# Output of the MLP by seven quarter products in two more batches, with the operand combinations of w2 kept in DRAM

## Chip, core, metric

One core of one Trainium2 chip (trn2), all data fp32. The metric is device time in microseconds (us) of one execution. The kernel before took 1165.28 us (median of three runs, 1165.25 to 1166.52). "Faster" or "slower" means a difference of over 2%.

The engines: TensorE (PE in the profile, with its weight loads as PEld), VectorE (DVE), ScalarE (ACT), GpSimd (POOL), and SyncE (SP), which here only issues DMA transfers.

## The reference, cut to what matters

```python
# attention of 4 batches x 8 heads, 768 tokens of 64, masked by equal hash buckets -> x (4, 768, 512)
X = np.fft.fft(np.fft.fft(x, axis=1), axis=2)
u = x + np.real(X)
un = (u - mean(u)) / sqrt(var(u) + 1e-6)
return u + np.maximum(un @ w_ch1, 0.0) @ w_ch2      # w1: 512 x 2048, w2: 2048 x 512
```

The kernel works batch by batch (0 to 3) and weaves the attention of the next batch between the mix and MLP of the current one. Most of the MLP is two matrix products: h = relu(w1 x) and o = h w2. The change concerns the second, o.

## The kernel before: the parts concerned

A product of two matrices that are cut 2 x 2 takes eight products of quarters, or seven if combinations of the quarters are formed by additions first. Seven cost TensorE an eighth less and give VectorE additions to do. Each product is summed up in a bank of PSUM; copying or adding it out of the bank, so that the next product can have it, is called evacuation here. The kernel before already computes h by seven quarter products in batches 1 to 3, and o in batch 3 only. Batches 1 and 2 compute o directly; one token tile T of 128 tokens is one accumulation over 8 blocks for each of two halves of the hidden units:

```python
def outer(b, T, u, rs, rows, tag, whole=True):
    ...
        ps = pt([P, w], ...)                       # one PSUM bank of 128 x 512
        for i, (hr, fc) in enumerate(rows):
            nc.tensor.matmul(ps, hr, w2[:, fc, cols], start=(i == 0), stop=(i == len(rows) - 1))
            if i % 4 == 3:
                yield                              # here the attention of the next batch steps in
        nc.vector.scalar_tensor_tensor(            # u += rs * ps: the only work of DVE per tile
            u[:, cols], ps, rs, u[:, cols], op0=ALU.mult, op1=ALU.add)
        if whole:
            store(b, T, u, cols)                   # GpSimd issues the DMA to the output
```

Batch 3 uses `outer7`, for a pair of token tiles (j, j+3) at a time. Its shape, with the seven products named by their operands:

```python
s1 = a21 + a22;  s3 = a11 - a21                # operand sums on DVE, 128 x 512 each
p1 = product(a11, B11)                         # 4 matmuls 128 x 256 into a PSUM bank
qq = copy(p1)                                  # ACT
a11 = s1 - a11                                 # DVE
p4 = product(a22, T4);   v_low  += rv * p4     # evacuation by DVE
p1 = product(a12, B21, p1)                     # accumulates into the bank of the first
u_low += ru * p1                               # DVE
a12 = a12 - a11                                # DVE
pa = product(s1, T1);    p5 = copy(pa)         # ACT
pb = product(s3, T3);    p7 = copy(pb)         # ACT
pb = product(a11, T2)
qq += pb; u_high += ru*qq; qq += p7; v_low += rv*qq; qq += p5; v_high += rv*qq    # DVE
pa = product(a12, B22, pa); u_high += ru * pa  # DVE
```

T1 to T4 are the combinations of w2's quarters. `combine()` formed them in SBUF when batch 3 began (16 additions of 128 x 512). w1's combinations were already handled otherwise: formed once in batch 0 (`quarters`), written to DRAM (`ad`), and fetched block by block into a ring of NR = 12 buffers.

Of the kernel before, what the change touches and what calls it, by code (L numbers as in the profile page):

```python
# [11 lines left out]
F32 = mybir.dt.float32  # L12
# [5 lines left out]
ALU = mybir.AluOpType  # L18
AX = mybir.AxisListType

P = 128
B, H, S, D = 4, 8, 768, 64
# [457 lines left out]
def _main(  # L480
# [27 lines left out]
    def wt(shape, dtype, tag, name, bufs=2):  # L508
        return work.tile(shape, dtype, tag=tag, name=name, bufs=bufs)
# [599 lines left out]
    NR = 12  # L1109
# [12 lines left out]
    side = [w1f[:, at + i * HALF : at + (i + 1) * HALF] for i in range(2)]  # L1122

# [23 lines left out]
    HD = DM // 2  # L1147
    t7 = {}

    def combine():  # L1150
        parts = []
        for tl in (*pks, *(wt([P, 2, S], F32, "t6", f"t7_{i}", 2) for i in range(2))):
            dims = "p a b c -> p (a b c)" if len(tl.shape) == 4 else "p a b -> p (a b)"
            flat = tl.rearrange(dims)
            parts += [
                flat[:, i * 2 * HD : (i + 1) * 2 * HD].rearrange("p (k n) -> p k n", k=2)
                for i in range(3)
            ]
        for half in range(2):
            sums = [[parts.pop() for _ in range(3)] for k in range(2)]  # L1160
            for k in range(2):
                r = half * HF // 2 + 2 * k
                (b11, b12), (b21, b22) = (
                    [w2[:, i : i + 2, n : n + HD] for n in (0, HD)] for i in (r, r + HF)
                )
                t1, t2, t4 = sums[k]
                nc.vector.tensor_tensor(t1, b12, b11, op=ALU.subtract)
                nc.vector.tensor_tensor(t2, b22, t1, op=ALU.subtract)
                nc.vector.tensor_tensor(t4, b21, t2, op=ALU.subtract)
                nc.vector.tensor_tensor(b12, b22, b12, op=ALU.subtract)  # L1170
                for kk in range(2):
                    t7[half, 2 * k + kk] = (
                        b11[:, kk], b21[:, kk], b22[:, kk], t4[:, kk],
                        t1[:, kk], t2[:, kk], b12[:, kk],
                    )

    def outer7(b, half, hall, ut, rs):
        def tile_sums(j):
            if half == 0:
                for T in (j, j + GT):  # L1180
                    rs[T] = spread(b, T, ut[T])
            a11, a12, a21, a22 = (
                hall[:, i, :, (j + g * GT) * P : (j + g * GT + 1) * P]
                for g in range(2) for i in range(2)
            )
            s1 = wt([P, HF // 2, P], F32, "qt", f"s1_{half}_{j}", 2)
            nc.vector.tensor_tensor(s1, a21, a22, op=ALU.add)
            nc.vector.tensor_tensor(a21, a11, a21, op=ALU.subtract)
            return a11, a12, a21, a22, s1

        nxt = tile_sums(0)
        for j in range(GT):
# [4 lines left out]
            def product(a, i, ps=None):  # L1197
                start = ps is None
                if start:
                    ps = pt([P, HD], f"o{b}_{half}_{j}_{i}")  # L1200
                for r in range(HF // 2):
                    nc.tensor.matmul(  # L1202
                        ps, a[:, r], t7[half, r][i], start=start and r == 0,
                        stop=r == HF // 2 - 1, skip_group_check=not start,
                    )
                return ps

            low, high = slice(0, HD), slice(HD, DM)
            tmp = wt([P, 3, HD], F32, "kt", f"tmp{half}_{j}", 2)

            def add(t, r, cols, src):
                nc.vector.scalar_tensor_tensor(
                    t[:, cols], src, r, t[:, cols], op0=ALU.mult, op1=ALU.add
                )


            p1 = product(a11, 0)
# [3 lines left out]
            p4 = product(a22, 3)  # L1221
            add(v, rv, low, p4)
            yield
            p1 = product(a12, 1, p1)
# [4 lines left out]
            pa = product(s1, 4)  # L1229
            nc.scalar.copy(p5, pa)  # L1230
            yield
            pb = product(s3, 6)
# [3 lines left out]
            pb = product(a11, 5)  # L1236
# [11 lines left out]
            pa = product(a12, 2, pa)  # L1248
            add(u, ru, high, pa)
            if half:  # L1250
                store(b, j, u, high)
            yield

    def mlp7(b):
# [4 lines left out]
        if b == B - 1:  # L1259
            combine()  # L1260
# [36 lines left out]
        for half in range(2):  # L1297
# [46 lines left out]
            if b == B - 1:  # L1344
                yield from outer7(b, half, hall, ut, rs)
                continue
            for T in range(NT):
                if half == 0:
                    rs[T] = spread(b, T, ut[T])
                rows = [  # L1350
                    (hall[:, i, r, T * P : (T + 1) * P], i * HF + half * HF // 2 + r)
                    for r in range(HF // 2) for i in range(2)
                ]
                yield from outer(b, T, ut[T], rs[T], rows, f"{half}_", half == 1)
# [3 lines left out]
    MIX += [2 + NT + NDC + 2 * (7 * HF // 4 + NT * HF // 4)] * (B - 1)  # L1358
    LEFT = 8

    def after(n, one, two):

        for i, _ in enumerate(one):
            if i >= n and (i - n) % 5 < 4:
                next(two, None)
            yield

# [25 lines left out]
    for b in range(B):  # L1393
# [41 lines left out]
        if b == 0:  # L1435
            other = after(2 + NT, other, chain(weights(w2, moe_w_ch2), quarters()))
# [47 lines left out]
```

## Time and profile before

| | before |
|---|---|
| time, median of 3 | 1165.28 us |
| profiled execution | 1170.13 us, mean granted clock 0.992 |
| o of batches 1 and 2, TensorE | 192 matmuls 128x512 |
| o of batch 3, TensorE | 168 matmuls 128x256 (seven quarter products) |
| GpSimd-issued transfers | 65 (25 weight reads, 40 output stores) |

The page gives busy time per engine, then the same in 40 slices, then groups of like instructions; its lines for PE, DVE and DMA are in the prediction below. Each fp32 matmul of the source leaves two records in the trace, so 192 matmuls are 384 records.

### The profile page before, as it was taken

Reading aid. Unit: us, or ns where it says so; the run is one execution under the profiler, and the core shown is the slowest. Engines: PE = TensorE matmul, PEld = TensorE weight load, DVE = VectorE, ACT = ScalarE, POOL = GpSimd, SP = SyncE. Lnnn points to the kernel's source line nnn. Section 1 sums busy time; section 2 is a strip of 40 time slices with the busy share of each in tenths; the row PEclk is TensorE's granted clock in tenths of the full one; section 3 lists DMA queues with packets and bytes.
Section 4 is the critical chain, followed back from the end, with each engine's and each line's share of the span. In section 5 each row is a group of like instructions: output and inputs, shape, how many; then the busy total and the mean of one; then the engine's idle time right before and its main releaser. Section 6 shows DMA issues by size and latency. Waiting matters only on the chain. (4 is left out here: it accounts for less than half of the span.)

```text
span 1168.2 us, 12778 instructions
## 1 busy us (share of the span) xinstructions
PE 1120.9 (96%) x4633; PEld 589.3 (50%) x4633; DVE 720.8 (62%) x1225; ACT 438.6 (38%) x822; POOL 63.2 (5%) x133
## 2 busy tenths in 40 slices
PE   7999889999999999999999999999999999999996
PEld 4444355454445445644444444554444444868675
DVE  4889949838447365883457753885634857645353
ACT  6777348623223113344224511345313420251330
POOL 1000001101100010020000000002000001010002
PEclk9999989999999999999999999999999999999999
DMA  9524124404112011022102311013101211130201
GB/s 270 158 68 127 36 71 164 150 4 151 52 41 55 9 32 36 19 70 80 27 19 68 91 36 50 15 46 94 41 1 41 63 32 36 37 96 4 72 19 39
DMA packets 117958, 73.67 MB, mean 63 GB/s; under 512 B 80128, under 2 KB 112000, under 8 KB 117888
## 3 DMA queue, kind: packets, MB, share of 16 engines
q1 hardware_dynamic: 110544, 52.98, 16.8%
q0 software_dynamic: 5776, 19.40, 5.0%
q8 instruction: 39, 0.64, 0.2%
q10 hardware_dynamic: 1568, 0.39, 0.2%
q14 instruction: 31, 0.25, 0.1%
HBM read 59.12 MB, written 13.63 MB: 62 GB/s over the span
## 5 line engine op out<-in xcount | busy, mean ns | idle before, releaser
L1065 PE MATMUL o<-w,h 128*128 128x512 f32 x576 | 254.9, 596 | 0.6 <-DVE rt L859 0.6
L819 ACT ACTIVATE pk<-sc 128x768 f32<-128x768 f32 x192 | 147.8, 808 | 152.0 <-PE sc L815 107.1
L1065 PEld LDWEIGHTS o<-w,h 128*128 128x128 f32 x576 | 106.7, 190 | 132.1 <-issue 125.3
L825 DVE SCALAR_TENSOR_TENSOR pk<-qb,kb,pk 128x768 f32<-128x768 bf16 x132 | 129.4, 1013 | 66.3 <-ACT pk L819 66.3
L815 PE MATMUL sc<-qt,kt 64*128 64x384 f32 x768 | 153.5, 503 | 0.9 <-ACT pk L819 0.9
L836 PE MATMUL oo<-pk,vn 128*64 128x385 f32 (+1 forms) x768 | 150.4, 502 | 1.9 <-DVE pk L825 1.8
L1290 PE MATMUL h_p<-x,w 128*128 128x384 f32 x384 | 140.2, 494 | 2.1 <-ACT qt L531 0.6
L898 DVE TENSOR_TENSOR acc<-acc,pk 128x1536 f32<-128x1536 f32 (+1 forms) x80 | 113.3, 1433 | 9.9 <-ACT pk L819 9.2
L1290 PE MATMUL h_p<-w 128*128 128x384 f32 x288 | 106.3, 492 | 2.9 <-ACT qt L531 1.7
L1290 PEld LDWEIGHTS h_p<-x,w 128*128 128x128 f32 x384 | 69.7, 190 | 56.5 <-ACT h L1322 3.4
L836 PEld LDWEIGHTS oo<-pk,vn 128*64 128x64 f32 x768 | 48.1, 137 | 92.3 <-issue 75.6
L815 PEld LDWEIGHTS sc<-qt,kt 64*128 64x128 f32 x768 | 67.1, 187 | 49.7 <-issue 25.4
L1083 PE MATMUL h<-x,w 128*128 128x384 f32 x256 | 88.6, 499 | 1.0 <-ACT kt L531 0.6
L1290 PEld LDWEIGHTS h_p<-w 128*128 128x128 f32 x288 | 53.1, 190 | 43.4 <-ACT qt L531 2.4
L1083 PEld LDWEIGHTS h<-x,w 128*128 128x128 f32 x256 | 48.1, 193 | 37.4 <-issue 5.0
L1070 DVE SCALAR_TENSOR_TENSOR u<-o,rs,u 128x512 f32<-128x512 f32 x14 | 10.5, 751 | 67.3 <-PE o L1065 61.6
L995 ACT COPY F<-cs 128x257 f32<-128x257 f32 (+1 forms) x32 | 10.9, 377 | 91.4 <-PE cs L988 91.4
L1202 PE MATMUL o<-w,h 128*128 128x256 f32 x192 | 44.7, 379 | 0.0
L1202 PEld LDWEIGHTS o<-w,h 128*128 128x128 f32 x192 | 36.5, 190 | 5.4
L531 ACT COPY qt<-trq 128x192 f32<-128x192 f32 x40 | 14.8, 427 | 61.7 <-DVE qt L529 61.7
L988 PE MATMUL cs<-ch,z 128*128 128x128 f32 (+3 forms) x192 | 32.7, 322 | 4.7 <-ACT kt L531 2.6
L926 POOL DMA_DIRECT2D out_dram<-w x20 | 11.1, 557 | 476.9 <-DVE w L1070 346.3
(169 smaller groups left out, 1261.7 us busy)
## 6 DMA issues: line engine op xcount, KB each, us to landing
w<-ad SPq DMA_DIRECT2D x168, 128.0 KB, 2.0
zraw<-in_moe_w_ch_dram POOLq DMA_DIRECT2D x21, 512.0 KB, 4.2
vn<-in_v_dram SPq DMA_DIRECT2D x32, 192.0 KB, 3.3
qn<-in_q_dram SPq DMA_DIRECT2D x31, 192.0 KB, 3.3
kn<-in_k_dram SPq DMA_DIRECT2D x31, 192.0 KB, 3.4
ad<-st SPq DMA_DIRECT2D x8, 512.0 KB, 3.7
ad<-w SPq DMA_DIRECT2D x24, 128.0 KB, 2.2
fraw<-in_moe_w_ch_dram SPq DMA_DIRECT2D x4, 512.0 KB, 9.2
```

Of the source, the lines that this page charges most:

```text
L531: nc.scalar.copy(dst, src)
L815: last[0] = nc.tensor.matmul(ps[:, h, 0:HALF], kt[rows, ks], qt[rows, qs], start=kb is not None, stop=True,)
L819: nc.scalar.activation(pk[:, g, :, 0:HALF], ps[:, :, 0:HALF], AF.Exp, scale=SCALE)
L825: nc.vector.scalar_tensor_tensor(w, qb[:, h].rearrange("p (g s) -> p g s", g=2), kb[:, h, c : c + 1], w, op0=ALU.is_equal, op1=ALU.mult,)
L836: nc.tensor.matmul(oos[g][h * D : (h + 1) * D, 0:w], nat["v", n][:, c, h, :], pk[:, g, h, 0:w], start=(c == 0), stop=(c == NT - 1),)
L898: nc.vector.tensor_tensor(acc[:, g], (first if c == 1 else acc)[:, g], new[:, g, :, 0:HALF], op=ALU.add,)
L926: nc.gpsimd.dma_start(out[b, s0 : s0 + 2 * w - 1 : 2, cols], src[at : at + w, cols])
L988: nc.tensor.matmul(ps[:, pc + 2 * lo : pc + 2 * hi - 1 : 2], z[:, cp, pc, par, t * P : (t + 1) * P], ch[:, cp, pc, lo:hi], start=(cp == 0) ...
L1065: nc.tensor.matmul(ps, hr, w2[:, fc, cols], start=(i == 0), stop=(i == len(rows) - 1))
L1083: nc.tensor.matmul(ps, w1[:, c, fc * P : (fc + 1) * P], x[:, c, g * HALF : (g + 1) * HALF], start=(c == 0), stop=(c == NDC - 1),)
L1202: nc.tensor.matmul(ps, a[:, r], t7[half, r][i], start=start and r == 0, stop=r == HF // 2 - 1, skip_group_check=not start,)
L1290: nc.tensor.matmul(ps, ring[n % NR][:, k], right[i][:, k], start=start and k == 0, stop=k == 1, skip_group_check=not start,)
```

## The change

The intent: o by seven quarter products in batches 1 and 2 as well. There all seven right operands have to be available three times, and w2 itself and its four combinations don't fit beside each other. So all seven blocks of each half (B11, B21, B22, T1 to T4, 512 KB each) are written to DRAM once, in batch 0 (`quarters2`), and fetched into w2's place for every half pass; the fetch for the next half pass is issued right after a block's last use. The diff, cut to its core:

```diff
-    NR = 12
+    NR = 9
@@ combine() goes, quarters2() comes
+    bd = tc.dram_tile([2, 7, P, HF // 2, HD], F32, name="bd")
+    right7 = [w2f[:, i * QB : (i + 1) * QB]... for i in range(7)]      # seven places in w2
+    def quarters2():
+        st = wt([P, 3, 4, HD], F32, "z", "st2", 1)
+        for half in range(2):
+            for i, rows, n in ((B11, lo, 0), (B21, hi, 0), (B22, hi, HD)):
+                nc.sync.dma_start(bd[half, i], w2[:, rows, n : n + HD])      # the plain copies
+            for r in range(HF // 2):
+                ...                                                        # t1 .. t4 on DVE, 128 x 256
+                nc.sync.dma_start(bd[half, T4:, :, r]..., st[:, r % 3])
+                yield
@@ outer7
+                if j == GT - 1 and (b < B - 1 or half == 0):
+                    nc.sync.dma_start(right7[i], bd[1 - half, i])
             if j < GT - 1:
                 nxt = tile_sums(j + 1)
-            pb = product(a11, 5)
+            def third():
+                add(u, ru, high, product(a12, B22, pa))
+            if b < B - 1:          # in batches 1 and 2 this product comes before a11 * T2
+                third()
+                yield
+            pb = product(a11, T2)
@@ mlp7
-            if b == B - 1:
-                yield from outer7(b, half, hall, ut, rs)
-                continue
-            for T in range(NT): ... yield from outer(...)
+            yield from outer7(b, half, hall, ut, rs)
@@ batch 0
-            other = after(2 + NT, other, chain(weights(w2, moe_w_ch2), quarters()))
+            other = after(2 + NT, other, chain(weights(w2, moe_w_ch2), quarters(), quarters2()))
```

More of the change, by code (lines that the diff above doesn't have):

```diff
@@ L1122, in _main @@
     side = [w1f[:, at + i * HALF : at + (i + 1) * HALF] for i in range(2)]
+    HD = DM // 2
+    temps = [
+        w1f[:, at + i * S : at + (i + 1) * S].rearrange("p (i n) -> p i n", n=HD)
+        for i in range(2)
+    ]
     def quarters():
@@ L1142, in quarters @@
             yield
-    HD = DM // 2
-    t7 = {}
-    def combine():
-        parts = []
-        for tl in (*pks, *(wt([P, 2, S], F32, "t6", f"t7_{i}", 2) for i in range(2))):
-            dims = "p a b c -> p (a b c)" if len(tl.shape) == 4 else "p a b -> p (a b)"
-            flat = tl.rearrange(dims)
-            parts += [
-                flat[:, i * 2 * HD : (i + 1) * 2 * HD].rearrange("p (k n) -> p k n", k=2)
-                for i in range(3)
-            ]
+    B11, B21, B22, T4, T1, T2, T3 = range(7)
+    bd = tc.dram_tile([2, 7, P, HF // 2, HD], F32, name="bd")
+    w2f = w2.rearrange("p c f -> p (c f)")
+    QB = HF // 2 * HD
+    right7 = [
+        w2f[:, i * QB : (i + 1) * QB].rearrange("p (r n) -> p r n", n=HD) for i in range(7)
+    ]
+    s1s = [
+        w2f[:, 7 * QB + i * HD * 2 : 7 * QB + (i + 1) * HD * 2].rearrange(
+            "p (r n) -> p r n", n=P
+        )
+        for i in range(2)
+    ]
+    def quarters2():
+        st = wt([P, 3, 4, HD], F32, "z", "st2", 1)
         for half in range(2):
-            sums = [[parts.pop() for _ in range(3)] for k in range(2)]
-            for k in range(2):
-                r = half * HF // 2 + 2 * k
+            lo, hi = (slice(i + half * HF // 2, i + (half + 1) * HF // 2) for i in (0, HF))
+            for i, rows, n in ((B11, lo, 0), (B21, hi, 0), (B22, hi, HD)):
+                nc.sync.dma_start(bd[half, i], w2[:, rows, n : n + HD])
+            for r in range(HF // 2):
                 (b11, b12), (b21, b22) = (
-                    [w2[:, i : i + 2, n : n + HD] for n in (0, HD)] for i in (r, r + HF)
+                    [w2[:, i + half * HF // 2 + r, n : n + HD] for n in (0, HD)]
+                    for i in (0, HF)
                 )
-                t1, t2, t4 = sums[k]
+                t4, t1, t2, t3 = (st[:, r % 3, i] for i in range(4))
                 nc.vector.tensor_tensor(t1, b12, b11, op=ALU.subtract)
@@ L1169, in combine @@
                 nc.vector.tensor_tensor(t4, b21, t2, op=ALU.subtract)
-                nc.vector.tensor_tensor(b12, b22, b12, op=ALU.subtract)
-                for kk in range(2):
-                    t7[half, 2 * k + kk] = (
-                        b11[:, kk], b21[:, kk], b22[:, kk], t4[:, kk],
-                        t1[:, kk], t2[:, kk], b12[:, kk],
-                    )
+                nc.vector.tensor_tensor(t3, b22, b12, op=ALU.subtract)
+                nc.sync.dma_start(
+                    bd[half, T4:, :, r].rearrange("i p n -> p i n"), st[:, r % 3]
+                )
+                yield
     def outer7(b, half, hall, ut, rs):
@@ L1185, in tile_sums @@
             )
-            s1 = wt([P, HF // 2, P], F32, "qt", f"s1_{half}_{j}", 2)
+            s1 = s1s[j % 2]
             nc.vector.tensor_tensor(s1, a21, a22, op=ALU.add)
@@ L1202, in product @@
                     nc.tensor.matmul(
-                        ps, a[:, r], t7[half, r][i], start=start and r == 0,
+                        ps, a[:, r], right7[i][:, r], start=start and r == 0,
                         stop=r == HF // 2 - 1, skip_group_check=not start,
                     )
+                if j == GT - 1 and (b < B - 1 or half == 0):
+                    nc.sync.dma_start(right7[i], bd[1 - half, i])
                 return ps
             low, high = slice(0, HD), slice(HD, DM)
-            tmp = wt([P, 3, HD], F32, "kt", f"tmp{half}_{j}", 2)
+            tmp = temps[j % 2]
             def add(t, r, cols, src):
@@ L1214, in add @@
                 )
-            p1 = product(a11, 0)
+            p1 = product(a11, B11)
             qq, p5, p7 = (tmp[:, i] for i in range(3))
@@ L1220, in outer7 @@
             nc.vector.tensor_tensor(a11, s1, a11, op=ALU.subtract)
-            p4 = product(a22, 3)
+            p4 = product(a22, T4)
             add(v, rv, low, p4)
             yield
-            p1 = product(a12, 1, p1)
+            p1 = product(a12, B21, p1)
             add(u, ru, low, p1)
@@ L1228, in outer7 @@
             nc.vector.tensor_tensor(a12, a12, a11, op=ALU.subtract)
-            pa = product(s1, 4)
+            pa = product(s1, T1)
             nc.scalar.copy(p5, pa)
             yield
-            pb = product(s3, 6)
+            pb = product(s3, T3)
             nc.scalar.copy(p7, pb)
@@ L1247, in outer7 @@
             yield
-            pa = product(a12, 2, pa)
-            add(u, ru, high, pa)
+            if b == B - 1:
+                third()
+                yield
             if half:
                 store(b, j, u, high)
-            yield
     def mlp7(b):
@@ L1258, in mlp7 @@
         )
-        if b == B - 1:
-            combine()
+        if b == 1:
+            for i in range(7):
+                nc.sync.dma_start(right7[i], bd[0, i])
         t1, t2, t4 = bs
@@ L1343, in mlp7 @@
                     yield
-            if b == B - 1:
-                yield from outer7(b, half, hall, ut, rs)
-                continue
-            for T in range(NT):
-                if half == 0:
-                    rs[T] = spread(b, T, ut[T])
-                rows = [
-                    (hall[:, i, r, T * P : (T + 1) * P], i * HF + half * HF // 2 + r)
-                    for r in range(HF // 2) for i in range(2)
-                ]
-                yield from outer(b, T, ut[T], rs[T], rows, f"{half}_", half == 1)
+            yield from outer7(b, half, hall, ut, rs)
     MIX = [2 + NT + NDC + 2 * (NFC + GT * NFC // 4)]
-    MIX += [2 + NT + NDC + 2 * (7 * HF // 4 + NT * HF // 4)] * (B - 1)
+    MIX += [2 + NT + NDC + 2 * (7 * HF // 4 + GT * 4)] * (B - 1)
     LEFT = 8
@@ L1366, in after @@
             yield
+        for _ in two:
+            pass
     other = weights(w1, moe_w_ch1)
```

## The prediction

> **What bounds the kernel now.** I read the page's busy shares and slices first, then the chain of waits, then stretches of the time by engine, then the timeline inside the stage that changes. The chain that ended last is of no use here: it holds only the last output transfer. Busy shares and slices:
>
> ```profile
> PE 1120.9 (96%) x4633; PEld 589.3 (50%) x4633; DVE 720.8 (62%) x1225; ACT 438.6 (38%) x822; POOL 63.2 (5%) x133
> ...
> PE   7999889999999999999999999999999999999996
> PEld 4444355454445445644444444554444444868675
> DVE  4889949838447365883457753885634857645353
> ...
> DMA  9524124404112011022102311013101211130201
> ```
>
> PE (TensorE) is at nine tenths or more in nearly every slice, DVE (VectorE) nowhere near that for long, DMA idle after the start. So the sum of TensorE's work sets the time, and what is not TensorE work counts only where it makes TensorE wait. The stretch of batches 1 and 2, with the tail (columns: stretch, us, then busy us of each engine):
>
> ```profile
> 491.90:766.00 274.10, 267.69 (x1064) 130.24 (x1063) 166.26 (x263) 96.97 (x180) 10.54 (x21) 1.00 0.19 50
> 766.00:1000.00 234.00, 230.71 (x847) 110.02 (x846) 142.56 (x235) 75.88 (x143) 10.54 (x21) 1.00 0.15 44
> ...
> 548.00:610.00 62.00, 61.91 (x215) 26.08 (x212) 28.91 (x39) 13.50 (x22) 0.00 (x0) 1.00 0.09 20
> 671.00:735.00 64.00, 63.49 (x230) 29.27 (x226) 32.08 (x55) 13.48 (x24) 4.56 (x9) 1.00 0.14 39
> ```
>
> The last two rows are the two halves of batch 1's output product o (before: full 128x512 matmuls) with the attention of batch 2 woven in. TensorE idles 0.6 us of 126 there, and DVE is busy 61 of 126: there is little waiting to win, only work, and DVE has about half its time free. What one matmul really costs is the distance between starts, not the mean of the group list, since they overlap:
>
> ```profile
> 692.83 27.73 PE L1065 MATMUL o<-w,h 128*128 128x512 f32 x64
> ...
> 720.40 1.05 PE L988 MATMUL cs<-ch,z 128*128 128x129 f32 x8
> ```
> ```profile
> 1055.21 1.89 PE L1202 MATMUL o<-t,s 128*128 128x256 f32 x8
> ...
> 1056.94 1.89 PE L1202 MATMUL o<-w,h 128*128 128x256 f32 x8
> ```
>
> From the first pair (720.40 - 692.83) / 64 = 0.431 us for one 512-wide record; from the second, in batch 3 which already uses seven products, (1056.94 - 1055.21) / 8 = 0.216 us for a 256-wide one. Each matmul of the source leaves two such records (batch 3: 2 halves x 3 tile pairs x 7 products x 4 = 168 matmuls; its groups count 192 + 48 + 48 + 24 + 24 = 336).
>
> **What the Trainium skill says.** "TensorE: Matmul & The Clock Gate", section Back-to-back issue gap, gives 518 cycles for 512 columns and 262 for 256: two halves cost only 1% more than one whole. The trace agrees (2 x 0.216 = 0.432 against 0.431), at twice the time per record because the data are fp32. "Perfetto Trace Analysis", section Identifying the Most-Contended Engine, says that matmul busy time is a poor measure of the distance to the limit; hence the starts above. Its section Matmuls wants independent groups to rotate through PSUM banks so that the evacuation of one overlaps the next: this is the point on which my prediction turns, because in batches 1 and 2 only two banks serve these products (batch 3 has six). "VectorE: DVE Perf Modes", section The TRN2 errata, gives (N+151)/0.96 ns for an fp32 add; 691 ns for 512 and 424 ns for 256. The trace has 690 ns and 416 to 425 ns.
>
> **The change part by part.**
> TensorE, batches 1 and 2. Removed per batch: 2 halves x 6 tiles x 8 = 96 matmuls, 192 records x 0.429 (0.431 with one attention switch or two) = 82.4 us. Added: 168 matmuls, 336 records x 0.216 = 72.6 us. Gain 9.8 us a batch, 19.6 us in both: 1.7% of 1165.3. That is all the arithmetic can give, and it is entirely on the bounding engine.
>
> DVE, batches 1 and 2. Per pair of tiles and half the old form has two 128x512 updates of 0.75 us. The new one has four 128x512 adds (0.69), six 128x256 scaled updates (0.483) and three 128x256 adds (0.42): 2.76 + 2.90 + 1.27 = 6.92 us against 1.50, so +5.4 us; six of them a batch: +32.5 us, +65 us in both. ACT gets three copies of 0.37 each: +13 us in both. Beside TensorE this fits: the stretch 548 to 610 becomes about 57 us long with 28.9 + 16.3 = 45.2 us of DVE (79%); 671 to 735 about 59 us with 48.4 (82%). So DVE doesn't become the bound on average, but its queue gets full.
>
> Forming the combinations. The sixteen-fold 128x512 work of `combine` (16 x 0.69 = 11 us of DVE, around 967 to 985) goes. In its place 32 adds of 128x256 (32 x 0.42 = 13.4 us of DVE) come in batch 0's mix, after the like combinations of w1 at about 293 us, where DVE is busy 9.2 and 6.1 of 20 us: hidden. Both were off the bounding engine, so about 0.
>
> Transfers. Written once: 14 blocks of 512 KB, 7.3 MB. Fetched: 7 blocks for each of six half passes, 42 x 512 KB = 22 MB. 512 KB lands in 3.7 to 4.4 us here; seven in a row are at most some 31 us. The block of the next half is asked for as soon as its last use in this half is over, and the h products in between last 61 us (610 to 671) in batches 1 and 2 and 37 us in batch 3; for batch 1 the place in w2 is free from 446 us and needed at 548. So hidden. The ring of w1 blocks falls from 12 to 9 places of 128 KB: at 4 records x 0.323 = 1.3 us a product that is still 11 us ahead of a landing of 2.0 us. Cost 0 to 2 us where a 512 KB block is queued in front.
>
> PSUM banks. This is the term that I have to estimate. The old outer product holds a bank for 16 records (6.9 us), and its evacuation may come up to 6.9 us late without harm. A quarter product is 8 records, 1.73 us; with two banks the evacuation of one must be done when the next ends. Four of the five evacuations per tile pair are DVE's, and DVE is in order behind the attention's work. One attention step in this stage, from the same trace:
>
> ```profile
> 580.99 1.56 PE L815 MATMUL sc<-qt,kt 64*128 64x384 f32 x8
> ...
> 583.55 1.95 DVE L825 SCALAR_TENSOR_TENSOR pk<-qb,kb,pk 128x768 f32<-128x768 bf16 x2 [5.14 <-ACT pk L819]
> ...
> 585.89 1.75 DVE L898 TENSOR_TENSOR acc<-acc,pk 128x1536 f32<-128x1536 f32 x1
> ```
>
> DVE is taken until 587.64, 6.65 us after the step began; TensorE is through with the step's own matmuls after 2.9 us. Two quarter products bring it to 6.4 us, then the third wants the first one's bank, which DVE frees at about 6.65 + 0.48 + 0.2 = 7.3. Depending on which of the four steps of a tile pair follows, I get 0, about 0.7, 0.3 to 1.9, and 0.6 us of waiting: some 0.5 us a step. An output stage is 24 of some 56 steps that are spread over 24 attention steps, so 10 attention steps a batch, less those left for the end: 18 in both batches, 18 x 0.5 = 9 us. I add 1 us for the transfers.
>
> Sum: -19.6 + 9 + 1 = about -10 us, 1155 us.
>
> **The rivals.** (a) Nothing waits: the scheduled order puts the evacuations ahead of the attention's adds, and the whole 19.6 us come out: 1146. For it: the h products live on the same two banks with 1.3 us of slack and the long stretch 491.9 to 766 shows TensorE idle only 6.4 us. Against it: those banks are emptied by ACT, whose queue is short there. (b) Evacuation on a full DVE takes the place of the work removed: 1 us or more per attention step and several at the normalising of a head pair (690.8 to 696.3, DVE without a break), 20 us or more: 1165 or slower. For it: DVE at 80% with pieces of up to 1.75 us against a slack of 1.73. Against it: the attention's own matmuls, 2.9 us, often stand between two quarter products and give DVE time. (c) The fetches come late: 512 KB blocks in front of the ring or of q, k and v: a wait of several us at six half passes, 1160 to 1175. Against it: DMA is at 0.09 to 0.19 of its capacity here. (d) More than the arithmetic: only if the shorter DVE-heavy stretch before batch 3 also gains; I see no more than 1 to 2 us.
>
> **Range and chances.** The floor is 1144 to 1146, no waits; I put the low end at 1146. The upper end is waits of 18 us, 1164. Faster by over 2% means below 1142, more than all the removed work: 2%. Slower by over 2% means above 1188.6, 42 us of waits: 3%. Within 2%: 95%.
>
> **What would show it.** Right: no 128x512 output records after batch 0, 1008 quarter records at 0.216 us apart; TensorE's busy time down by less than 20 us; DVE up by some 65 us; short TensorE gaps of 0.3 to 2 us inside the output stages of batches 1 and 2, released by DVE's scaled updates, none in batch 3; time in the h stages unchanged. Wrong: gaps before the quarter products that end with a transfer (rival c); no gaps at all (a); gaps that add up to over 18 us (b); a longer batch 0, which would mean that forming the combinations isn't hidden.

## The result, and the profile after

| | before | after |
|---|---|---|
| median of the runs taken together | 1165.9 us (1165.25 to 1170.73, 4 runs) | 1154.97 us (1154.21 to 1155.47, 4 runs) |
| ratio of the fast runs | | 0.9897, 95% interval 0.9869 to 0.9924: within 2% |
| output correct | yes | yes |

A ratio is the mean time of one kernel's fast runs over that of the other's of the same rounds, so it isn't quite the ratio of the medians quoted beside it.

The page after, with the lines that answer to those of before:

```profile
PE 1100.6 (96%) x4921; PEld 641.9 (56%) x4921; DVE 779.9 (68%) x1373; ACT 451.8 (39%) x858; POOL 74.5 (6%) x149
...
DVE  4889959837938455883857877785775877644352
...
DMA  9534135514611014113042315013104204131401
...
L1214 PE MATMUL o<-w,h 128*128 128x256 f32 x864 | 194.0, 381 | 0.0
...
w<-bd SPq DMA_DIRECT2D x42, 512.0 KB, 4.4
```

TensorE is busy 20 us less and DVE 59 us more than on the page before. (Against the second trace of before, introduced below, in which TensorE was busy 1115.8 us, it is 15 us less; busy time is not the work, as the prediction says.) The added DVE work shows in the slices of batches 1 and 2 (20th to 34th). The 42 fetches of `bd` land in 4.4 us (median). All of that is near what was predicted (for DVE, some 65 us). What the page doesn't tell is whether the total of about -10 us came about in the predicted way, as -19.6 + 9 + 1. For that I compared traces.

First, a caution about which traces. The first trace of before is of a long execution (1170.13 us). I took a second one of the same kernel later (run `d0_before_trace`, 1165.16 us). Two stretches of both, in batch 0; columns are the stretch, its length, busy us of PE, PEld, DVE, ACT, POOL with instruction counts, then PEclk, the share of full TensorE clock that was granted:

```profile
150.00:162.00 12.00, 9.32 (x43) 4.87 (x43) 4.96 (x5) 4.83 (x10) 0.00 (x0) 0.72 0.37 87
224.00:242.00 18.00, 15.98 (x53) 8.66 (x53) 11.74 (x20) 9.38 (x20) 1.05 (x2) 0.91 0.34 114
```
```profile
150.00:162.00 12.00, 9.39 (x61) 5.73 (x60) 5.78 (x7) 5.71 (x12) 0.00 (x0) 1.00 0.28 67
224.00:242.00 18.00, 17.34 (x66) 9.24 (x67) 9.33 (x18) 6.84 (x13) 1.05 (x2) 1.00 0.27 81
```

The first fence is the long execution, the second the short one. PEclk (the third number from the end) is below 1 in the long one alone. The records there show the clock at one half for 3.4 us, or twice that: 6.8 us at half clock in 12 us gives 0.72, 3.4 us in 18 gives 0.91. A further 3.4 us at half clock, at 128 us, are in both executions. The Trainium skill, "TensorE: Matmul & The Clock Gate", section What's actually happening, says that TensorE's clock is halved after an idle window of about 3.4 us and that this window runs freely, without being reset when a kernel starts. The traces agree on the length and on the free running: in the first one the halved stretches begin at 129.02, 152.91 and 228.01 us, 7 and 22 times 3.41 us apart, and the same kernel meets them in other places from run to run. They don't agree that the window is idle: in the 3.4 us before these three beginnings TensorE's records cover 34%, 46% and 41% of the time. Of the 35 runs of the kernel before whose clock is on record, the 13 with mean clock 0.998 took 1164.5 to 1165.5 us and the 8 with 0.992 took 1169.5 to 1170.7. The two traces account for it: 13.6 us at half clock are 6.8 us of lost clock, 3.4 us are 1.7, and the two executions are 5.0 us apart. (The mean clock also counts time at half clock after the last matmul, 4.6 us of it in `d0_before_trace`, which costs nothing.) So I compare traces that have these stretches in the same places, or name the difference.

The cleanest pair is `d0_before_trace` against the second trace of after (`c0_after_again`, 1155.26 us): both have one half-clock stretch, at 128 us, before the difference begins. The attention's score matmuls are the same 768 records in both kernels, so the start of the n-th one is a clock for comparing them:

| start of score record n | before, us | after, us | difference | where this is |
|---|---|---|---|---|
| 256 | 188.2 | 188.5 | +0.3 | batch 0, ahead of its MLP |
| 288 | 258.3 | 263.4 | +5.1 | batch 0, in its MLP |
| 480 | 550.5 | 556.0 | +5.5 | batch 1, o begins |
| 512 | 600.9 | 602.4 | +1.5 | half of o of batch 1 |
| 640 | 761.8 | 759.3 | -2.5 | between the o stages |
| 736 | 908.0 | 901.3 | -6.7 | batch 2, ahead of the second half of o |
| last matmul | 1153.5 | 1142.3 | -11.2 | end of batch 3 |
| end of span | 1163.2 | 1153.4 | -9.8 | |

Each of the four half stages of o gives 4.0 to 4.5 us. But 5 us are lost in batch 0, where nothing was predicted, and 1.4 us after the last matmul. The sum comes out right because its errors cancel. The rest of the work was to find out what each of the three pieces is.

**The o stages.** I added up, in the traces, the distance from each output record of batches 1 and 2 to the next TensorE record. Before: 384 records, 167.9 us, of which 384 x 0.429 = 164.8 are the floor and 3.1 are extra. After: 672 records, 151.6 us, of which 672 x 0.216 = 145.2 are the floor and 6.5 extra. So the work fell by 19.6 us, the prediction's number, but the extra grew by only 3.4 us where it had 9 us of waits. Not all of the 3.4 is waiting: 2.6 us, in seven places of both batches, end with one of DVE's scaled updates; the rest is more of the 0.1 us steps that stand in both kernels at changes to or from the attention's matmuls. The load of DVE in the first half stage of batch 1, `d0_before_trace` and then after, and under it the last half stage of batch 2 in after:

```profile
543.40:600.80 57.40, 57.30 (x190) 24.30 (x188) 26.58 (x36) 10.96 (x18) 0.00 (x0) 1.00 0.09 21
```
```profile
547.60:601.40 53.80, 53.45 (x262) 37.77 (x260) 38.05 (x62) 13.79 (x27) 0.00 (x0) 1.00 0.24 72
...
932.70:975.90 43.20, 43.03 (x205) 34.18 (x204) 33.18 (x70) 6.18 (x14) 7.03 (x13) 1.00 0.25 83
```

DVE is busy 38.05 of 53.80 us, 71%; the prediction had 79% for this stage. But the waits don't simply follow this load: the four half stages have loads of 71, 75, 71 and 77% and extras of 1.9, 1.9, 1.8 and 0.9 us, so the fullest one has the least. What TensorE's output products waited for in the whole kernel after (columns: who ended the idle time, us, times):

```profile
L1214 PE MATMUL o<-w,h x864: 379/379/483, 547.7 to 1141.3; 128*128 128x256 f32 x173
...
its engine sat idle before it (us, times) until:
  issue: 4.6, 8
  DVE u L1226: 2.3, 2
...
  DVE w L1226: 1.6, 4
```

At most six waits of these products end with one of DVE's scaled updates (L1226). The list counts weight loads and matmuls separately, so one wait can be in it twice. The largest one lies behind the normalising of a head pair, where the prediction had seen DVE without a break:

```profile
691.28 0.55 DVE L869 TENSOR_TENSOR x<-x,rb 128x384 f32<-128x384 f32 x1
691.75 1.01 DVE L825 SCALAR_TENSOR_TENSOR pk<-qb,kb,pk 128x768 f32<-128x768 bf16 x1
692.68 0.48 DVE L1226 SCALAR_TENSOR_TENSOR u<-o,rs,u 128x256 f32<-128x256 f32 x1
...
693.21 1.99 PE L1214 MATMUL o<-w 128*128 128x256 f32 x8 [0.93 <-DVE u L1226]
```

DVE runs the attention's instructions one after the other (each starts before the one ahead of it has ended: 691.75 + 1.01 is later than 692.68), and only then the update that frees the bank. In an ordinary attention step it is the other way round:

```profile
577.14 1.95 DVE L825 SCALAR_TENSOR_TENSOR pk<-qb,kb,pk 128x768 f32<-128x768 bf16 x2 [1.50 <-ACT pk L819]
...
577.50 1.99 PE L1214 MATMUL o<-w 128*128 128x256 f32 x8
...
579.12 1.76 DVE L898 TENSOR_TENSOR acc<-acc,pk 128x1536 f32<-128x1536 f32 x1
...
579.33 3.62 PE L1214 MATMUL o<-w,h 128*128 128x256 f32 x16
...
579.55 0.36 ACT L1244 COPY w<-o 128x256 f32<-128x256 f32 x1
581.26 0.37 ACT L1247 COPY w<-o 128x256 f32<-128x256 f32 x1 [1.35 <-PE o L1214]
...
582.99 0.48 DVE L1226 SCALAR_TENSOR_TENSOR w<-o,rs,w 128x256 f32<-128x256 f32 x1 [2.11 <-PE o L1214]
```

This is the step for which the prediction assumed some 0.5 us of waiting. Three quarter products (8 + 16 records) run on without a gap while DVE masks and adds for 3.7 us; the first two are emptied by ACT. Then DVE itself stands idle for 2.11 us until TensorE is done.

**Batch 0.** In the trace of after, between 226 and 237 us, DVE, then TensorE:

```profile
228.18 0.69 DVE L607 SCALAR_TENSOR_TENSOR w<-zraw,w 128x512 int32<-128x512 int32 x1
230.93 0.43 DVE L603 TENSOR_SCALAR w<-zraw 128x512 int32<-128x512 int32 x1 [2.06 <-DMA zraw<-in_moe_w_ch_dram]
...
234.01 0.43 DVE L603 TENSOR_SCALAR w<-zraw 128x512 int32<-128x512 int32 x1 [1.45 <-DMA zraw<-in_moe_w_ch_dram]
...
235.56 0.55 DVE L1089 TENSOR_SCALAR h<-h 128x384 f32<-128x384 f32 x1
```
```profile
236.16 6.15 PE L1083 MATMUL h<-x,w 128*128 128x384 f32 x13 [3.13 <-DVE h L1089]
```

DVE waits twice for a transfer that brings weights (zraw). Behind that in its queue is the relu of h (L1089), and TensorE waits 3.13 us for it. In before (`d0_before_trace`) the same wait was 0.66 us:

```profile
233.36 5.43 PE L1083 MATMUL h<-x,w 128*128 128x384 f32 x16 [0.66 <-DVE h L1089]
```

What stands in those transfers' way is on SP's queue, again in after:

```profile
225.20 1.24 SPq L1173 DMA_DIRECT2D bd<-w  x2
...
274.41 1.25 SPq L1173 DMA_DIRECT2D bd<-w  x2
```

These are four of the six plain copies of w2's quarters to DRAM (L1173); the first two are issued at 188.7 and 208.8 us. In the program they come after `quarters()`, but they need nothing but w2, so they were scheduled as soon as the rows they read were there, between the last reads of weights. GpSimd issues the last two weight reads at 224.78 and 226.32 us; two copies of 512 KB each are issued from 225.20 us on. From issue to landing, these two reads take 6.1 and 7.7 us; in `d0_before_trace` they take 5.1 and 4.9, and in d2 below, where the copies come later, 4.6 each. And the wait has a second price. The stretches around it, for after:

```profile
224.00:232.00 8.00, 7.78 (x24) 4.48 (x24) 4.94 (x11) 4.14 (x9) 1.06 (x2) 1.00 0.81 234
232.00:236.20 4.20, 1.07 (x10) 0.20 (x9) 2.75 (x6) 1.56 (x4) 0.00 (x0) 1.00 0.39 148
236.20:242.00 5.80, 5.80 (x13) 3.36 (x14) 0.38 (x1) 0.49 (x1) 0.00 (x0) 0.71 0.00 0
```

The DMA share (the number after PEclk) is 0.81 where it is 0.60 in `d0_before_trace`; then TensorE is idle for 3.1 of 4.2 us; then its clock is halved for 3.4 us, which makes 0.71 over 5.8 us and costs another 1.7 us. A wait of 3.1 us became a loss of about 5.

**The end.** After the last matmul nothing differs but the end of GpSimd's program: a drain instruction of its sequencer, visible in the trace though not in the views, takes 5381 ns before and 6765 ns after. GpSimd issued 65 transfers before and 81 after. The group of output stores in the page after:

```profile
L926 POOL DMA_DIRECT2D out_dram<-w x30 | 16.5, 552 | 468.7 <-issue 426.6
```

with 26 more that store from u. 56 stores and 25 weight reads are 81. Before there were 40 stores, because a tile was stored as one piece of 512 columns; seven quarter products finish the two column halves apart, and the change stores them apart.

### The profile page after: what moved, and what is told of

The parts are those of the page before. It is cut to its first block, busy times and chain, and to the rows that moved or that the text cites. A ratio compares the mean times of both kernels' runs of the same rounds, so it can differ in the third digit from the quotient of the medians.

```text
span 1152.4 us, 13749 instructions
## 1 busy us (share of the span) xinstructions
PE 1100.6 (96%) x4921; PEld 641.9 (56%) x4921; DVE 779.9 (68%) x1373; ACT 451.8 (39%) x858; POOL 74.5 (6%) x149
## 5 line engine op out<-in xcount | busy, mean ns | idle before, releaser
L1214 PE MATMUL o<-w,h 128*128 128x256 f32 x864 | 194.0, 381 | 0.0
L1214 PEld LDWEIGHTS o<-w,h 128*128 128x128 f32 x864 | 162.3, 190 | 30.2 <-issue 3.4
L1065 PE MATMUL o<-w,h 128*128 128x512 f32 x192 | 85.2, 596 | 0.6 <-DVE rt L859 0.6
L1065 PEld LDWEIGHTS o<-w,h 128*128 128x128 f32 x192 | 35.5, 190 | 43.8 <-issue 41.7
L926 POOL DMA_DIRECT2D out_dram<-w x30 | 16.5, 552 | 468.7 <-issue 426.6
L1226 DVE SCALAR_TENSOR_TENSOR w<-o,rs,w 128x256 f32<-128x256 f32 x42 | 20.1, 481 | 32.2 <-PE o L1214 32.2
L1244 ACT COPY w<-o 128x256 f32<-128x256 f32 x18 | 6.7, 372 | 81.7 <-PE o L1214 81.7
L1214 PE MATMUL o<-w 128*128 128x256 f32 x144 | 34.6, 383 | 1.2 <-DVE u L1226 0.9
```

Of the source, the lines that this page charges most:

```text
L926: nc.gpsimd.dma_start(out[b, s0 : s0 + 2 * w - 1 : 2, cols], src[at : at + w, cols])
L1214: nc.tensor.matmul(ps, a[:, r], right7[i][:, r], start=start and r == 0, stop=r == HF // 2 - 1, skip_group_check=not start,)
L1226: nc.vector.scalar_tensor_tensor(t[:, cols], src, r, t[:, cols], op0=ALU.mult, op1=ALU.add)
```

## The experiments

The theory: the result is -19.6 us of TensorE work, +3.4 between the output records (2.6 of it waits on evacuation), +5 lost in batch 0 by the early copies, +1.4 by the drain. The rivals are the prediction's own: (b) evacuation behind a full DVE is what eats the gain, (c) the fetches do. In most diffs `b < B - 1` means batches 1 and 2; batch 0 doesn't come here.

**c0_after_again: the changed kernel once more.** No edit.

> The changed kernel itself, again, as the mark for the other runs of this chip. Both theories: a ratio to the kernel before of 0.990 (0.987 to 0.992), about 1155 us.

Measured 1154.15 us (1153.07 to 1157.19, 5 runs), ratio 0.9905 (0.9889 to 0.9920). The gain stands, and this is the trace of the ledger above.

**c1_late_copies: the plain copies held back until the combinations of w1 are stored.**

```diff
-            nc.sync.dma_start(ad[f, 3:7]..., st[:, f % 3])
+            stored[0] = nc.sync.dma_start(ad[f, 3:7]..., st[:, f % 3])
...
-                nc.sync.dma_start(bd[half, i], w2[:, rows, n : n + HD])
+                with tc.issue_after(stored[0].ins):
+                    nc.sync.dma_start(bd[half, i], w2[:, rows, n : n + HD])
```

> The changed kernel with the copies of w2's three plain quarters queued behind the stores of w1's combinations, so that none stands among the last reads of w2. Theory A (these copies delay the last weight reads, VectorE waits for them, and TensorE loses 3.2 us at about 232 us): 3 us shorter than the changed kernel, about 1152 us, and the 3.1 us gap of the h matmuls before the VectorE's relu is gone. Rival (the gap is chance of that one trace, or comes from VectorE's new work or the clock): within 1 us of the changed kernel.

Measured 1153.73 us (1150.92 to 1155.34, 5 runs), ratio 0.9898 (0.9883 to 0.9914): not told apart from c0 by the times. The trace shows that the wait in batch 0 is gone. But three of the five runs had a mean clock of 0.991, against 0.994 and 0.996 for the other two, and the halved clock took back what the wait had cost. Its run at 0.996 took 1150.92 us, where the run of c0 at 0.996 took 1153.43. So: the mechanism confirmed, the size not. Why this kernel met the halved clock more often in these runs was not traced and stays open.

**c2_before_plus_store: the kernel before, with `quarters2` added in batch 0 and its result never used.**

```diff
+    def quarters2(): ...                     # as in the change, word for word
-            other = after(2 + NT, other, chain(weights(w2, moe_w_ch2), quarters()))
+            other = after(2 + NT, other, chain(weights(w2, moe_w_ch2), quarters(), quarters2()))
```

> The kernel before, which in batch 0 also forms w2's combinations and stores all seven blocks, and never uses them. Theory A: 3 us longer than the kernel before, about 1168.5 us, with VectorE waiting for the last weight reads. Rival (forming and storing is hidden, as predicted): within 1 us of the kernel before.

Measured 1170.54 us (1169.88 to 1172.26, 6 runs) against 1165.19 of before in the same rounds: ratio 1.0044 (1.0032 to 1.0056), +5.3 us. This is the cost of writing the blocks to DRAM, by itself, with o computed the old way. The prediction had it at about 0. In the trace TensorE waits for the relu of h, and the halved clock follows, as in after:

```profile
236.94 1.74 PE L1083 MATMUL h<-x,w 128*128 128x384 f32 x3 [2.70 <-DVE h L1089]
```

**c3_no_sums: the four operand sums of a tile pair left out in batches 1 and 2** (the output is wrong; everything else runs as it did).

```diff
-            nc.vector.tensor_tensor(s1, a21, a22, op=ALU.add)
-            nc.vector.tensor_tensor(a21, a11, a21, op=ALU.subtract)
+            if b == B - 1:
+                nc.vector.tensor_tensor(s1, a21, a22, op=ALU.add)
+                nc.vector.tensor_tensor(a21, a11, a21, op=ALU.subtract)
@@ and likewise for the sums into a11 and a12
```

> Wrong result on purpose: in batches 1 and 2 the four 128x512 operand sums of a tile pair are left out, 12 x 2.76 = 33 us less VectorE work in the output stages, the products and their evacuations as before. If VectorE's queue is what holds the two PSUM banks: the output stages lose up to 2.6 us of TensorE waits, 1153 us or a little less. If the waits are what the prediction made of them (9 us): about 1148 us. If VectorE's load does not matter there: 1155 us.

Measured 1153.22 us (1152.02 to 1156.61, 5 runs), ratio 0.9901 (0.9885 to 0.9917). The times say no difference from c0. The sum over the 672 output records is 149.8 us against 151.6: 1.8 us less. Taking 33 us of work off DVE (48 additions of 0.69 us) is worth 1.8 us, so rival (b) can't be where most of the missing gain is.

**d0_before_trace: the kernel before, one look,** for a trace of a fast execution.

> The kernel before, unchanged, for a second trace: the first one was of a run with 1170.13 us and a granted clock of 0.992, where 15 other runs have 1164.5 to 1167.8 us and 0.995 to 0.998. Expected about 1165.2 us, 0.998, and no stretch at half clock inside batch 0; TensorE then reaches the first h matmul of batch 1 about 5 us sooner than in the first trace.

Measured 1165.16 us at clock 0.997. (A single run, so its state is unknown; its time is that of the runs of before at 0.997 to 0.998.) It is used throughout.

**d1_whole_stores: in batches 1 and 2 a tile is stored whole again, when its second column half is done.**

```diff
-            if half:
+            if half and b == B - 1:
                 store(b, j, u, low)
...
-                store(b, j + GT, v, high)
+                store(b, j + GT, v, high if b == B - 1 else slice(0, DM))
```

> The changed kernel with whole rows stored in batches 1 and 2 once both column halves are done, as the kernel before does: 65 transfers issued by GpSimd as before, and not 81. If GpSimd's last drain (5.38 us before, 6.76 us after) grows with the number of its transfers: drain back at 5.4 us and the time 1.4 us below the changed kernel, about 1153 us. If the drain has another cause: 1154.5 us, drain 6.8.

Measured 1153.34 us (1152.32 to 1156.39, 6 runs), ratio 0.9886 (0.9866 to 0.9905). GpSimd issues 65 transfers again, the drain is 5381 ns again, and from the start of the last matmul to the end of the span it takes 9.7 us instead of 11.1. The 1.4 us of the tail are shown by the trace; on the clock of the runs alone, whose spread is larger, they would not be.

**d2_late_copies_whole_stores: both.** The edits of c1 and d1 together.

> Both: plain copies queued after w1's combinations, whole rows stored. If both costs are real and separate: 1154.2 - 3.2 - 1.4 = 1149.6 us at the clock of the changed kernel; each further 3.4 us stretch at half clock in batch 0 adds 1.7 us, as the late copies alone seem to have met. If late copies bring nothing that lasts: 1152.5 us.

Measured 1148.25 us (1147.98 to 1151.72, 5 runs, clocks 0.995 to 0.998), ratio 0.9845 (0.9823 to 0.9866), output correct. Against d1 of the same rounds that is -5.1 us, which is the cost of the early copies, taken away. DVE and TensorE at the place of the old wait:

```profile
229.39 0.43 DVE L603 TENSOR_SCALAR w<-zraw 128x512 int32<-128x512 int32 x1 [0.62 <-DMA zraw<-in_moe_w_ch_dram]
...
232.48 0.55 DVE L1089 TENSOR_SCALAR h<-h 128x384 f32<-128x384 f32 x1
```
```profile
233.08 5.43 PE L1083 MATMUL h<-x,w 128*128 128x384 f32 x16 [0.17 <-DVE h L1089]
```

The relu comes at 232.48 instead of 235.56 us, and TensorE's wait is 0.17 us. The clock stays up as well:

```profile
232.00:236.20 4.20, 4.03 (x19) 2.08 (x19) 1.54 (x3) 0.23 (x1) 0.00 (x0) 1.00 0.00 0
236.20:242.00 5.80, 5.80 (x27) 2.91 (x26) 1.60 (x3) 1.06 (x2) 0.00 (x0) 1.00 0.01 3
```

On the ledger by score records d2 is at -0.3 us at record 288 and at -16.9 at the last matmul and at the end: the whole gain of the o stages, nothing given back. The sum over its 672 output records is 151.6 us, the same as in c0 and d1.

**d3_more_dve: the first operand sum formed five times over in batches 1 and 2,** so that DVE has 33 us more to do there.

```diff
-            nc.vector.tensor_tensor(s1, a21, a22, op=ALU.add)
+            for _ in range(5 if b < B - 1 else 1):
+                nc.vector.tensor_tensor(s1, a21, a22, op=ALU.add)
```

> The changed kernel with one operand sum of each tile pair formed five times over in batches 1 and 2 (same result): 12 x 4 x 0.69 = 33 us more VectorE work in the output stages, which would then be busy there some 85% in place of 71%. If evacuation behind VectorE's queue is what the small waits are: TensorE's waits in these stages grow by several us, 1157 to 1165 us. If VectorE has slack there to spare: within 1 us of the changed kernel.

Measured 1160.87 us (1160.64 to 1161.17, 4 runs), ratio 0.9945 (0.9922 to 0.9968): +6.7 us over c0's median, which is of other rounds. The traces of d3 and after, with the half clock in the same place, are also 6.7 us apart (spans 1159.1 and 1152.4). The output records add up to 158.4 us, 6.8 more than in c0. The first half stage of batch 1 and the wait list, which can be held against those of after:

```profile
547.40:603.40 56.00, 53.50 (x262) 37.69 (x260) 43.30 (x74) 13.82 (x27) 0.00 (x0) 1.00 0.23 70
```
```profile
its engine sat idle before it (us, times) until:
  DVE w L1227: 7.3, 6
```

DVE is at 77% (43.30 of 56.00) and the waits for its scaled updates (here L1227) are 7.3 us in the list where they were 1.6 and 2.3. The extra over the floor is 158.4 - 145.2 = 13.2 us against 3.1 before, a growth of 10.1. Of the 13.2, 5.7 us end with a scaled update (2.6 in after) and 3.9 with a step of the attention's normalising (L859). So the mechanism of the prediction is real: work in front of an evacuation does hold TensorE. The size near its 9 us shows nothing about its estimate, though. Waits follow the place of the work and not the load alone: d3 adds four additions in one row per tile pair, and its half stages at 77, 86, 77 and 87% have extras of 4.1, 2.3, 4.3 and 2.5 us, where after had 0.9 at 77%.

**f0_batch2_only: seven products from batch 2 on, the old `outer` in batch 1.**

```diff
-        if b == 1:
+        if b == 2:
             for i in range(7):
                 nc.sync.dma_start(right7[i], bd[0, i])
...
+            if b == 1:
+                for T in range(NT): ... yield from outer(...)
+                continue
             yield from outer7(b, half, hall, ut, rs)
```

> The changed kernel with the old 512-wide output in batch 1 and the seven products from batch 2 on: half the dose. From the ledger of the traces: batch 0 keeps its whole cost (3.2 us of waiting and 1.7 us of half clock), one batch brings 8.4 us, GpSimd has 8 transfers more than before (0.7 us): 1165.2 + 5 + 0.7 - 8.4 = 1162.5 us. If the gain were not the sum of equal batches (say a warm-up or a pace effect of the whole): away from this by more than 2 us.

Measured 1161.65 us (1161.10 to 1162.66, 4 runs), ratio 0.9954 (0.9927 to 0.9981). The fixed cost in batch 0 is paid in full, half of the gain is had. The 336 output records of the one batch add up to 75.2 us, half of the 151.6.

**f1_no_refetch: the 35 fetches after the first seven left out** (wrong; the products run on stale blocks).

```diff
-                if j == GT - 1 and (b < B - 1 or half == 0):
+                if False:
                     nc.sync.dma_start(right7[i], bd[1 - half, i])
```

> Wrong result on purpose: the changed kernel without the 35 later fetches of w2's blocks (18 MB), so that each half pass uses the first half's blocks. If the fetches are hidden, as predicted: within 1 us of the changed kernel, 1154 us. If they delay the ring of w1 blocks or q, k and v (rival c): 2 us or more below it.

Measured 1154.39 us (1153.47 to 1155.89, 4 runs), ratio 0.9887 (0.9860 to 0.9914): the time of the changed kernel. 18 MB less fetched change nothing that can be seen; rival (c) falls.

**f2_before_ring9: the kernel before with NR = 9,** the other side effect of the change.

> The kernel before with 9 in place of 12 places in the ring of w1 blocks. If 9 are deep enough (a landing of 2.0 us against 5.8 us of products at the fastest): within 1 us of 1165.2 us. If not: longer, with TensorE waiting for transfers in the h stages.

Measured 1166.03 us (1164.96 to 1168.22, 4 runs) against 1166.26, ratio 0.9986 (0.9959 to 1.0014). The smaller ring costs nothing.

**f3_gpsimd_sums: d2, with two of the four operand sums moved to GpSimd in batches 1 and 2,** to see whether the remaining waits can be had.

```diff
-            nc.vector.tensor_tensor(a21, a11, a21, op=ALU.subtract)
+            eng = nc.vector if b == B - 1 else nc.gpsimd
+            eng.tensor_tensor(a21, a11, a21, op=ALU.subtract)
@@ likewise a12 - a11
```

> The best version so far (late copies, whole stores, 1148.3 us) with two of the four operand sums of a tile pair on GpSimd in batches 1 and 2: 12 x 1.38 = 17 us less VectorE work in these stages. If GpSimd forms a sum within the time of the products that lie before its use (3.5 us or more): up to 1 us shorter. If its sums take longer than that or slow VectorE: longer, with TensorE waiting for them.

Measured 1155.21 us (1150.60 to 1156.87, 6 runs, three of them at clock 0.992), ratio 0.9887 (0.9861 to 0.9912). Its one run at clock 0.998 took 1150.6 us; the two runs of d2 at 0.998 took 1148.1 and 1148.0. So it is slower by about 2.5 us even with the clock set aside, and its output records add up to 154.7 us, 3.1 more. The sums on GpSimd, then the sum that stayed on DVE (durations min/median/max):

```profile
L1204 POOL TENSOR_TENSOR h<-h 128x512 f32<-128x512 f32 x12 | 18.1, 1514 | 201.9 <-DVE w L1202 201.9
L1247 POOL TENSOR_TENSOR h<-h 128x512 f32<-128x512 f32 x12 | 15.5, 1289 | 93.7 <-PE o L1218 83.5 <-DVE h L1238 10.1
```
```profile
L1202 DVE TENSOR_TENSOR w<-h x18: 683/693/1773, 545.9 to 1115.9; 128x512 f32<-128x512 f32 x18
```

GpSimd takes 1.3 to 1.5 us (its times in a profile are rough) for an addition that takes DVE 0.69, and the addition on DVE takes up to 1.77 us. The Trainium skill, "SBUF — State Buffer", section Who interferes with whom, says that a DVE instruction with two inputs in SBUF contends with GpSimd instructions that read SBUF, because its second input comes through an interface they share. This trace agrees: the longest `L1202` is 2.6 times the median, the three of over 1.7 us all began while a GpSimd addition (L1204) was running, and no such spread appeared while GpSimd had no additions (621 to 693 ns for 66 of them in d3).

## Why the prediction was right, and where it wasn't

The time was right (1155 predicted, 1154.97 measured) and so was the class. The sum behind it was not, in three of its terms, and that they cancel was luck. Predicted: -19.6 + 9 + 0 + 1 = -10. Measured, in the pair of like traces: -19.6 + 3.4 + 5.1 + 0 + 1.4 = -9.7, and the spans differ by 9.8.

- **TensorE's work, -19.6: right.** 384 records at 0.429 us against 672 at 0.216: 164.8 - 145.2 = 19.6. The step that carried it was to take the distance between starts from records of the shape that the change would use, which batch 3 already had, and not the 381 ns that the group's mean shows.
- **PSUM banks, +9: the wait is real, its size wrong.** The term that failed is "some 0.5 us a step", times 18 steps. The extra came out at 3.4 us, of which 2.6 us, in seven places, are waits for a scaled update. The step that it was built on is not the kernel's: "the third wants the first one's bank, which DVE frees". In the step at 577.50 ACT empties the first two products, and the third, which the diff puts between T3 and T2, accumulates into the first one's bank as soon as ACT has copied it out; it asks nothing of DVE. "Four of the five evacuations" leaves out what the prediction itself had counted: of the seven products of a tile pair ACT copies out three. That this order is why most steps don't wait is argued from the trace; no run tried the other order. The load was also put too high: "45.2 us of DVE (79%)" for the first half stage, where 38.05 of 53.80 us (71%) was measured. Of the 7.2 us between them some 4 are work of the three tile pairs that lies before or after the stretch, 2 are attention work that no longer falls into it, and 0.8 are DVE instructions that overlap. But the load is not what the waits follow (d3 and the four half stages of after), and c3, which takes 33 us of DVE work away, gains only 1.8.
- **Forming and storing the combinations, "hidden: about 0": wrong.** This cost 5 us: +5.1 in the ledger, +5.3 in c2, where it is done alone, and -5.1 from d1 to d2, where the cause is taken away. The prediction checked that DVE had time for the additions, and it had. It took the transfers for "written once: 7.3 MB" and asked only whether they come in time to be fetched, not what they would stand in front of. Six copies that depend on nothing but w2 were issued among the last weight reads, a conversion waited for its weights, a relu stood behind that conversion in DVE's queue, and TensorE behind the relu. The prediction did name a longer batch 0 as what would show it wrong, and that is where it showed.
- **Fetches and the ring, "0 to 2 us": right at its low end.** f1 and f2 show nothing.
- **The end of the kernel, +1.4: not thought of.** 16 more stores by GpSimd, found in the ledger's last row and taken away by d1.
- **The rivals.** (a), no waits at all, 1146, is nearly what d2 reaches (1148.25) once the two side costs are gone; the 3.4 us of extra remain. (b) and (c) fall by c3 and f1. (d) didn't occur.

So the error of -5.6 in the waits met errors of +5.1 and +1.4 that weren't foreseen, less the 1 us put down for transfers. A right total is no proof of the parts, and without the comparison of traces this prediction would have passed for understood. It also hid 6 us: d2, the changed kernel with late copies and whole stores, takes 1148.25 us, the fastest and correct, 1.5% below before.

## What to carry to other kernels

When a change adds transfers that nothing waits for, ask what they are issued in front of: here the scheduler placed them as early as their inputs allowed, among the last loads of something urgent, and the in-order queue of DVE passed the delay on to TensorE, where a wait of 3.1 us also halved the clock for 3.4 us. Don't estimate waits from an engine's load in a stage: here the half stage with the highest load, 77%, waited least. Follow each bank from its product to the engine that empties it, in the order of the kernel that will run. And compare two traces record by record at work that both kernels share: the place where the difference changes shows what a sum that happens to be right conceals.

## What the Trainium skill lacked or had wrong

- No page has the drain at the end of GpSimd's program: 5381 ns after 65 GpSimd-issued transfers (six traces), 6111 after 73 (f0) and 6764 or 6765 after 81 (six traces), at the very end of the span where nothing hides it. That is 86.5 ns for each further transfer on the mean. The number of transfers is not all: f3, with 65 and 24 additions on GpSimd, has 5458.
- "TensorE: Matmul & The Clock Gate", section Back-to-back issue gap, has no row for fp32 in its table (the number of passes that fp32 takes stands elsewhere in the skill). Here each matmul leaves two records, with starts 0.216 us apart at 256 columns and 0.429 at 512; each record is about twice as long as the page's figure for its columns.
- The same page, section What's actually happening, calls the cost of the clock's ramp under 1% of a span. That holds, but a tuned kernel is compared at that size: the same kernel took 1164.5 to 1165.5 us at a mean clock of 0.998 and 1169.5 to 1170.7 at 0.992, and a wait of 3.1 us in the middle of the kernel cost 1.7 us more through the halved clock. The "idle window" that the section names need not be idle: before the halving at 228.01 us of the first trace TensorE was busy 41% of 3.4 us, and its longest wait there was 1.45 us.
- "TensorEngine Tiling (Array Packing)", section Key Properties, says that a change of tiling mode drains TensorE and gives no number. Here the first full 128x128 record after one on part of the array took 483 ns instead of 379 at 256 columns, 104 ns more (ends of matmuls are modelled in the trace, but the next record also starts 0.1 us later). In batches 1 and 2 of the changed kernel 17 of the 21 such long output records follow directly on a record with a smaller array tile; in the kernel before, 13 of 13 (697 ns instead of 592 at 512 columns).
